# Chunked attention and two dense layers on one core: head order in the loads, GpSimd's share of the first block, and attention ahead of the in-projection

## The chip, the cores and the metric

One core of a Trainium2 chip. The core has TensorE (PE in the profile; its weight loads are PEld), VectorE (DVE), ScalarE (ACT), GpSimd (POOL) and SyncE (SP), which here issues every DMA. The metric is the device time of one execution, in microseconds, as the median of the runs shown.

## The reference

q, k and v have 4 batches, 8 heads, 576 positions and 64 values a head. Attention is computed within chunks of 64 positions only. Its result, heads side by side, is a matrix of 2304 tokens by 512, which goes through two dense layers of the same shape, each with an in-projection to 2048, an activation and an out-projection back to 512:

```
scores = 1/sqrt(64) * (q_c @ k_c.T)          # per batch, head and chunk of 64
attn   = exp(scores - max) / (sum + 1e-9)
x      = (attn @ v_c), heads side by side     # 2304 x 512
x      = gelu_sigmoid(x @ w_in1) @ w_out1     # h * 1/(1+exp(-1.702 h))
out    = mish(x @ w_in2) @ w_out2             # h * tanh(softplus(h))
```

The weights come as 64-bit floats, q, k and v as 32-bit floats.

## The kernel before

Tokens are worked on in six blocks of 384 (three attention tiles of 128 tokens each). A block of a layer has 16 units n, one for each 128 of the 2048 inner columns (f = n % 16). A unit is an in-projection into a PSUM tile h (12 matmuls: four slices of the depth, and for each the products high x high, low x high and high x low of 32-bit numbers split in two, `mm3`), the activation t on ACT, its high part gh and its remainder gl, and two units later (`LAG`) an out-projection of 12 matmuls into the accumulators acc. The first layer's six blocks come first, then the second layer's. The engines' queues are filled in the order in which the code is written (`manual_schedule`), and each engine works strictly in its order.

Weights. Each 64-bit weight tile (512 KB, "raw") is loaded, scaled on ACT (`scale`), put together from its two halves on VectorE in two instructions (`join`, L151 and L152), and split: the high part wi or wo on ACT (L173), the low part by a subtraction (L174), which before stands on GpSimd. One call of `convert` does a split, a join, a scale and further loads for successive tiles. In block 0 of the first layer each unit calls it twice, since every weight is first needed there; the second layer's weights are joined during later blocks and parked in DRAM (`staged`), and split late in the first layer's last block. Raw tiles go through five rotating buffers once the spare ones are used up.

Attention. A tile of 128 tokens is two chunks for eight heads. Its steps are `transposes` of q and k (PSUM tr), the copies qt and kt, `scores` (sc), `shift` (maximum mx and subtraction into e), `exp`, `sums` (sm, rc), `normalize`, `attn_t` (transposes of e, PSUM at) with the copy a, `pv`, then `x_hi` (xh) and `x_lo` (xl), the halves of the layer's input. Matmuls of 64 by 64 use a half of the rows (the row start of the operands) and a half of the columns (the row start of the output). The first three tiles and the first weights follow a list written by hand (`PLAN`); the others are spread over units: f = 1, 6, 11 transposes and the loads of the tile after next, f = 2, 7, 12 scores to normalization, f = 4, 9, 14 attn_t, f = 5, 10, 15 pv to xl. All four PSUM results of a tile share one slot outside the list. In block 0 the normalization and gl stand on GpSimd, in later blocks on VectorE.

Loads. Before, q and k of a tile come in two transfers each (heads 0 to 3, heads 4 to 7, interleaved in SBUF), and v in four of 64 KB, so that each chunk's heads lie in a half of the partitions.

Of the kernel before, what the change touches and what calls it, by code (L numbers as in the profile page):

```python
# [16 lines left out]
P = 128  # L17
# [18 lines left out]
def tile_kernel(  # L36
# [40 lines left out]
    class Weights:  # L77
# [8 lines left out]
        def __init__(self, w_in, w_out, staged):  # L86
# [5 lines left out]
            self.raw, self.f32, self.hi, self.lo = {}, {}, {}, {}  # L92
            self.first, self.ahead = 0, NRAW - 2 if staged else NRAW
# [72 lines left out]
        def split(self):  # L166
# [46 lines left out]
    def load_values(t, i):  # L213

        for c in range(2):
            b, s = divmod(i * P + c * CH, S)
            for r in range(2):
                nc.sync.dma_start(
                    out=t[r * CH : (r + 1) * CH].rearrange("k (p c d) -> k p c d", c=2, d=D)[:, :, c],
                    in_=v[b, r * NP : (r + 1) * NP, s : s + CH, :].rearrange("p k d -> k p d"),  # L220
                )

    class Attention:
# [31 lines left out]
        def scores(self):  # L255
            self.pt = pt = self.psum("sc")
            for p in range(NP):
                for c in range(2):
                    c0 = p * P + c * CH
                    cs = slice(c * CH, (c + 1) * CH)  # L260
                    for r in range(2):
                        rs = slice(r * CH, (r + 1) * CH)
                        nc.tensor.matmul(
                            pt[cs, r, p * CH : (p + 1) * CH],
                            self.qt[rs, c0 : c0 + CH],
                            self.kt[rs, c0 : c0 + CH],
                            start=True,
                            stop=True,
                        )

        def shift(self):
            if self.e is None:
                self.e = at.tile([P, DM], F32, tag="q", name=f"e{self.i}")
            self.eg = self.e.rearrange("p (g k) -> p g k", g=G)
            sv = self.pt[:, :, 0 : NP * CH].rearrange("p r (h k) -> p r h k", h=NP)
            mx = st.tile([P, 2, NP, 1], F32, tag="mx", name=f"mx{self.i}")
            nc.vector.reduce_max(out=mx, in_=sv, axis=AX.X)
            nc.vector.tensor_tensor(
                out=self.e.rearrange("p (h r k) -> p r h k", h=NP, r=2),
                in0=sv,  # L280
                in1=mx.to_broadcast([P, 2, NP, CH]),
# [28 lines left out]
        def pv(self):  # L310
            self.pt = pt = self.psum("pv")
            for p in range(NP):
                for c in range(2):
                    w, o = p % 2, p // 2 * P + c * CH
                    vs = slice((2 * p + c) * D, (2 * p + c + 1) * D)
                    qs = slice(p * P + c * CH, p * P + (c + 1) * CH)
                    for r in range(2):
                        rs = slice(r * CH, (r + 1) * CH)
# [332 lines left out]
```

## Time and profile before

| | |
|---|---|
| median of 3 runs | 895.48 us (894.75 to 896.47) |
| profiled execution, its own time | 894.35 us |
| its span (first to last instruction) | 892.4 us |
| PE busy | 869.9 us, 97% of the span |
| DVE busy | 355.6 us, 40% |
| ACT busy | 276.8 us, 31% |
| POOL busy | 115.0 us, 13% |
| granted TensorE clock, mean | 0.996 of full speed |

Busy shares are means over stages with different limits; the profile also gives them by stretches of time, for each line of the kernel, and as waits with what ended them. A time such as 28.11 counts from the first instruction of the profiled execution.

### The profile page before, as it was taken

The numbers are of one execution on the slowest core, as the hardware profiler recorded it, in microseconds if no ns is written. First come the engines' busy times: TensorE is split into PE (matmuls) and PEld (weight loads), VectorE is DVE, ScalarE is ACT, GpSimd is POOL, SyncE is SP. The second block draws the span as 40 slices with busy tenths as digits, with TensorE's granted clock in tenths as the row PEclk, the third lists the DMA queues.
The fourth block names the chain that finished last, engine by engine and source line by source line (L and its number), as shares of the span: only waits on it lengthen the run. The fifth ranks groups of instructions, "written<-read, shape, count | busy, mean of one in ns | idle before, by whom it ended". The sixth has DMA issues, their size and how long they took to land.

```text
span 892.4 us, 13796 instructions
## 1 busy us (share of the span) xinstructions
PE 869.9 (97%) x5724; PEld 812.1 (91%) x5724; DVE 355.6 (40%) x633; ACT 276.8 (31%) x469; POOL 115.0 (13%) x92
## 2 busy tenths in 40 slices
PE   7878999999999999999999999999999999999998
PEld 5777899999999999999999999999999999999997
DVE  5789744445445455445333222222222222222221
ACT  4777733333334343333434111111111111111111
POOL 2688700000000000000565000000000000000000
PEclk9999999999999999999999999999999999999999
DMA  8957724455336435523342000300200200200000
GB/s 208 284 163 218 213 96 107 107 139 181 117 96 195 125 107 169 153 71 128 112 127 83 1 1 1 107 1 1 106 1 1 107 1 1 107 1 1 36 1 36
DMA packets 93406, 82.69 MB, mean 93 GB/s; under 512 B 60320, under 2 KB 76704, under 8 KB 93344
## 3 DMA queue, kind: packets, MB, share of 16 engines
q1 hardware_dynamic: 93344, 81.81, 31.0%
q8 instruction: 45, 0.74, 0.3%
q14 instruction: 17, 0.14, 0.1%
HBM read 62.39 MB, written 19.40 MB: 92 GB/s over the span
## 4 chain that ended last, share of the span: by engine, by line
PE 88%; DVE 4%; DMA 3%; ACT 2%; SPq 2%; issue 1%; POOL 0%; DVEq 0%; POOLq 0%; ACTq 0%
PE h L345 14%; PE h L343 14%; PE h L344 14%; PE acc L343 7%; PE acc L344 6%; PE acc L345 6%; PE accb L435 5%; PE accb L434 5%; PE accb L433 5%; PE third L434 3%; PE third L435 2%; PE third L433 2%; DVE raw L152 2%; DVE raw L151 2%; PE tr L247 1%
## 5 line engine op out<-in xcount | busy, mean ns | idle before, releaser
L365 DVE CAST gh<-t 128x384 fp32r<-128x384 f32 x176 | 69.3, 394 | 476.0 <-ACT t L413 296.1
L343 PE MATMUL h<-xh,wi 128*128 128x384 f32 x512 | 172.0, 336 | 1.9 <-ACT t L361 1.8
L345 PE MATMUL h<-xh,wi 128*128 128x384 f32 x512 | 171.9, 336 | 0.6 <-POOL wi L174 0.6
L344 PE MATMUL h<-xl,wi 128*128 128x384 f32 x512 | 171.3, 335 | 0.0
L413 ACT ACTIVATE t<-h 128x384 f32<-128x384 f32 x96 | 47.2, 492 | 335.2 <-PE h L345 334.4
L343 PE MATMUL acc<-gh,wo 128*128 128x384 f32 x384 | 134.1, 349 | 0.0
L344 PE MATMUL acc<-gl,wo 128*128 128x384 f32 x384 | 128.6, 335 | 0.0
L345 PE MATMUL acc<-gh,wo 128*128 128x384 f32 x384 | 128.5, 335 | 0.0
L370 DVE TENSOR_TENSOR gl<-t,gh 128x384 fp32r<-128x384 f32 x176 | 98.3, 559 | 11.8
L361 ACT ACTIVATE t<-h 128x384 f32<-128x384 f32 x96 | 47.1, 491 | 172.3 <-PE h L345 81.3
L343 PEld LDWEIGHTS h<-xh,wi 128*128 128x128 f32 x512 | 96.1, 188 | 4.6 <-ACT t L361 3.2
L344 PEld LDWEIGHTS h<-xl,wi 128*128 128x128 f32 x512 | 96.1, 188 | 1.3
L345 PEld LDWEIGHTS h<-xh,wi 128*128 128x128 f32 x512 | 96.1, 188 | 0.9 <-POOL wi L174 0.9
L345 PE MATMUL h<-x2h,wi 128*128 128x384 f32 x256 | 86.4, 337 | 0.0
L343 PE MATMUL h<-x2h,wi 128*128 128x384 f32 x256 | 86.2, 337 | 0.0
L344 PE MATMUL h<-x2l,wi 128*128 128x384 f32 x256 | 86.0, 336 | 0.0
L435 PE MATMUL accb<-wo,gl 128*128 128x512 f32 x192 | 76.2, 397 | 0.0
L434 PE MATMUL accb<-wo,gh 128*128 128x512 f32 x192 | 75.8, 395 | 0.0
L433 PE MATMUL accb<-wo,gh 128*128 128x512 f32 x192 | 74.6, 389 | 0.0
L343 PEld LDWEIGHTS acc<-gh,wo 128*128 128x128 f32 x384 | 72.1, 188 | 2.0
L344 PEld LDWEIGHTS acc<-gl,wo 128*128 128x128 f32 x384 | 72.2, 188 | 0.0
L345 PEld LDWEIGHTS acc<-gh,wo 128*128 128x128 f32 x384 | 72.1, 188 | 0.0
(85 smaller groups left out, 1052.5 us busy)
## 6 DMA issues: line engine op xcount, KB each, us to landing
raw<-in_moe_w_in_dram SPq DMA_DIRECT2D x32, 512.0 KB, 4.1
raw<-in_moe_w_out_dram SPq DMA_DIRECT2D x32, 512.0 KB, 4.0
w_f<-wf SPq DMA_DIRECT2D x32, 256.0 KB, 2.2
ws<-w_f SPq DMA_DIRECT2D x32, 256.0 KB, 2.7
v<-in_v_dram SPq DMA_DIRECT2D x72, 64.0 KB, 2.9
out_dram<-o SPq DMA_DIRECT2D x18, 256.0 KB, 2.1
q<-in_q_dram SPq DMA_DIRECT2D x26, 128.0 KB, 4.2
k<-in_k_dram SPq DMA_DIRECT2D x26, 128.0 KB, 4.3
```

The costliest lines, as they stand in the source:

```text
L151: nc.vector.tensor_scalar(lo, lo, 29, None, op0=ALU.logical_shift_right)
L152: nc.vector.scalar_tensor_tensor(to, hi, 3, lo, op0=ALU.logical_shift_left, op1=ALU.bitwise_or)
L343: nc.tensor.matmul(o, wh, mh, start=start, stop=False)
L344: nc.tensor.matmul(o, wh, ml, start=False, stop=False)
L345: nc.tensor.matmul(o, wl, mh, start=False, stop=stop)
L361: nc.scalar.activation(gt[n], hp.pop(n), AF.Gelu_apprx_sigmoid)
L365: (nc.scalar.copy if n < KF else nc.vector.tensor_copy)(gh[n], gt[n])
L370: eng.tensor_tensor(out=gl[n], in0=gt.pop(n), in1=gh[n].bitcast(F32), op=ALU.subtract)
L413: nc.scalar.activation(gt[n], h, AF.Mish)
L433: nc.tensor.matmul(o, a[:, ts], wh, start=f == 0, stop=False)
L434: nc.tensor.matmul(o, a[:, ts], wl, start=False, stop=False)
L435: nc.tensor.matmul(o, b[:, ts], wh, start=False, stop=f == KF - 1)
```

## The change

Loads: q, k and v of a tile each come in one transfer with the heads in their own order (two where a tile crosses a batch), and v lies by token like q and k. Scores and pv are addressed accordingly: scores take two head pairs to the two halves of the output's partitions, and pv reads a chunk's half of the rows and writes head parity to the halves of the output's partitions. The normalization and gl are on VectorE everywhere, and so is the low part of the first layer's split; that part is held back (`open`) until `rest`, which `convert` calls after its join. In block 0 gl of a unit is held back too (`late`) to the next unit, after its first `convert`. In each unit of the loop the attention step stands ahead of the in-projection. The list `PLAN` and the second layer's splits are as they were.

```diff
         def load_ahead(self):
-            used = self.at["join" if self.staged is not None else "split"]
+            used = self.at["join"] if self.staged is not None else self.at["split"] - len(self.open)
...
             nc.scalar.copy(hi, w)
-            nc.gpsimd.tensor_tensor(out=lo, in0=w, in1=hi.bitcast(F32), op=ALU.subtract)
-            self.hi[key], self.lo[key] = hi, lo
+            self.hi[key] = hi
+            self.open.append((key, w, hi, lo))
+            if self.staged is not None:
+                self.rest()
+
+        def rest(self):
+            eng = nc.vector if self.staged is None else nc.gpsimd
+            while self.open:
+                key, w, hi, lo = self.open.pop(0)
+                eng.tensor_tensor(out=lo, in0=w, in1=hi.bitcast(F32), op=ALU.subtract)
+                self.lo[key] = lo
+
+        def parts(self, key):
+            if key not in self.lo:
+                self.rest()
+            return self.hi[key], self.lo[key]
         def convert(self):
...
             if self.at["scale"] > self.at["join"]:
                 self.join()
+            self.rest()
...
-            for r in range(2):
-                nc.sync.dma_start(
-                    out=t[done : done + n].rearrange("t (p r d) -> t p r d", r=2, d=D)[:, :, r],
-                    in_=src[b, r * NP : (r + 1) * NP, s : s + n, :].rearrange("p t d -> t p d"),
-                )
+            nc.sync.dma_start(
+                out=t[done : done + n].rearrange("p (h d) -> p h d", h=H),
+                in_=src[b, :, s : s + n, :].rearrange("h p d -> p h d"),
+            )
...
-            self.v = at.tile([P, H * D], F32, tag="v", name=f"v{self.i}")
-            load_values(self.v, self.i)
+            self.v = load_tok(at, "v", v, self.i)
...
-            for p in range(NP):
+            for u in range(NP // 2):
                 for c in range(2):
-                    c0 = p * P + c * CH
-                    cs = slice(c * CH, (c + 1) * CH)
-                    for r in range(2):
...
-                            pt[cs, r, p * CH : (p + 1) * CH],
+                    o = (u * 2 + c) * CH
+                    for w in range(2):
+                        c0 = (2 * u + w) * P + c * CH
+                        for r in range(2):
...
+                                pt[w * CH : (w + 1) * CH, r, o : o + CH],
...
-                    w, o = p % 2, p // 2 * P + c * CH
...
+                    cs = slice(c * CH, (c + 1) * CH)
                     for r in range(2):
-                        rs = slice(r * CH, (r + 1) * CH)
+                        h = 2 * p + r
+                        o = (r * NP // 2 + p // 2) * P + p % 2 * CH
                         nc.tensor.matmul(
-                            pt[w * D : (w + 1) * D, r, o : o + CH],
-                            self.v[rs, vs],
-                            self.a[rs, qs],
+                            pt[r * D : (r + 1) * D, c, p * CH : (p + 1) * CH],
+                            self.v[cs, h * D : (h + 1) * D],
+                            self.a[cs, o : o + CH],
...
-        eng = nc.gpsimd if n < KF else nc.vector
-        eng.tensor_tensor(out=gl[n], in0=gt.pop(n), in1=gh[n].bitcast(F32), op=ALU.subtract)
+        nc.vector.tensor_tensor(out=gl[n], in0=gt.pop(n), in1=gh[n].bitcast(F32), op=ALU.subtract)
...
-            "U": lambda i: tiles[i].normalize(pool),
+            "U": lambda i: tiles[i].normalize(nc.vector),
...
         for n in range(4, N + LAG):
             f = n % KF
-            if n < NA:
-                j = n // KF
-                hp[n] = in_proj(W[0], (xh[j], xl[j]), f)
-                if n < KF:
-                    W[0].convert()
-                gelu(n)
-                g_hi(n)
-                g_lo(n)
...
             if n < NA - KF and f > 0:
...
+            if n < NA:
+                j = n // KF
+                hp[n] = in_proj(W[0], (xh[j], xl[j]), f)
+                if n < KF:
+                    W[0].convert()
+                while late:
+                    g_lo(late.pop())
+                gelu(n)
+                g_hi(n)
+                if n < KF:
+                    late.append(n)
+                else:
+                    g_lo(n)
```

What that does to VectorE's queue in the hand-written list, around the normalization of the second and third tile (e_201 is the second tile's e after the change, e_first the third's in both). Before, from the third tile's maximum on:

```order
L277 TENSOR_REDUCE mx_251<-sc_226 128x8
L278 TENSOR_TENSOR e_first<-sc_226,mx_251 128x2x4x64
L151 TENSOR_SCALAR raw_174<-raw_174 128x512
L152 SCALAR_TENSOR_TENSOR raw_174<-raw_174 128x512
L291 TENSOR_REDUCE sm_286<-e_first 128x8
L292 TENSOR_SCALAR sm_286<-sm_286 128x8
L293 RECIPROCAL rc_287<-sm_286 128x8
L151 TENSOR_SCALAR raw_203<-raw_203 128x512
L152 SCALAR_TENSOR_TENSOR raw_203<-raw_203 128x512
L151 TENSOR_SCALAR raw_221<-raw_221 128x512
L152 SCALAR_TENSOR_TENSOR raw_221<-raw_221 128x512
L339 TENSOR_TENSOR xl_387<-pv_315,xh_386 128x4x128
```

After, the same place from the first join on (maximum and shift of the third tile stand ahead of it as before; lines of the changed file):

```order
L152 TENSOR_SCALAR raw_168<-raw_168 128x512
L153 SCALAR_TENSOR_TENSOR raw_168<-raw_168 128x512
L301 TENSOR_REDUCE sm_274<-e_first 128x8
L302 TENSOR_SCALAR sm_274<-sm_274 128x8
L303 RECIPROCAL rc_275<-sm_274 128x8
L152 TENSOR_SCALAR raw_197<-raw_197 128x512
L153 SCALAR_TENSOR_TENSOR raw_197<-raw_197 128x512
L152 TENSOR_SCALAR raw_212<-raw_212 128x512
L153 SCALAR_TENSOR_TENSOR raw_212<-raw_212 128x512
L307 TENSOR_TENSOR e_201<-e_201,rc_237 128x512
L307 TENSOR_TENSOR e_first<-e_first,rc_275 128x512
L348 TENSOR_TENSOR xl_366<-pv_300,xh_365 128x2x4x64
```

The second tile's normalization, which was GpSimd's next instruction after the reciprocal, now stands on VectorE behind the third tile's shift, three joins and a sum.

VectorE in unit 5, the first with a pv in the loop. Before, xl and a run of joins:

```order
L339 TENSOR_TENSOR xl_732<-pv_714,xh_731 128x4x128
L151 TENSOR_SCALAR raw_612<-raw_612 128x512
L152 SCALAR_TENSOR_TENSOR raw_612<-raw_612 128x512
L151 TENSOR_SCALAR raw_652<-raw_652 128x512
L152 SCALAR_TENSOR_TENSOR raw_652<-raw_652 128x512
```

After, each join is followed by the subtraction of a split (wi, wo), and once a unit by a gl:

```order
L348 TENSOR_TENSOR xl_677<-pv_659,xh_676 128x2x4x64
L152 TENSOR_SCALAR raw_583<-raw_583 128x512
L153 SCALAR_TENSOR_TENSOR raw_583<-raw_583 128x512
L185 TENSOR_TENSOR wi_693<-raw_363,wi_693 128x512
L378 TENSOR_TENSOR gl_701<-t_635,gh_637 128x384
L152 TENSOR_SCALAR raw_631<-raw_631 128x512
L153 SCALAR_TENSOR_TENSOR raw_631<-raw_631 128x512
L185 TENSOR_TENSOR wo_719<-raw_583,wo_719 128x512
```

A split's subtraction stands one join behind the join of its own weight, and xl moved ahead of one join more.

ACT in unit 4, which has the copy a. Before, a stands behind the unit's gelu (t) and gh:

```order
L173 CAST wi_646<-raw_380 128x512
L141 ACTIVATE raw_384<-raw_384 128x512
L361 ACTIVATE t_654<-h_633 128x384
L365 CAST gh_656<-t_654 128x384
L308 COPY a_665<-at_660 128x512
```

After, a is the first instruction of the unit:

```order
L318 COPY a_610<-at_605 128x512
L174 CAST wi_625<-raw_359 128x512
L142 ACTIVATE raw_363<-raw_363 128x512
L370 ACTIVATE t_635<-h_612 128x384
L374 CAST gh_637<-t_635 128x384
```

The copies qt and kt, exp and xh moved in the same way in their units.

## Rows read from the trace of the kernel before

**Rows 1.** The page: busy time (parts 1) and a load's landing (part 6).
```profile
PE 869.9 (97%) x5724; PEld 812.1 (91%) x5724; DVE 355.6 (40%) x633; ACT 276.8 (31%) x469; POOL 115.0 (13%) x92
...
raw<-in_moe_w_in_dram SPq DMA_DIRECT2D x32, 512.0 KB, 4.1
```
**Rows 2.** Busy time by stretches: PE, PEld, DVE, ACT, POOL, PEclk, DMA share, GB/s.
```profile
28.11:43.75 15.64, 14.26 (x107) 12.99 (x106) 12.63 (x13) 13.65 (x23) 10.95 (x9) 1.00 1.06 328
43.75:54.34 10.59, 7.07 (x42) 6.43 (x41) 10.11 (x10) 7.33 (x12) 10.12 (x8) 1.00 0.58 143
54.34:82.31 27.97, 24.45 (x197) 23.03 (x197) 24.69 (x28) 21.54 (x38) 21.21 (x16) 1.00 0.68 199
82.31:110.00 27.69, 24.55 (x197) 23.10 (x197) 23.62 (x24) 20.55 (x36) 21.82 (x17) 1.00 0.78 222
```
**Rows 3.** The chain in block 1, 130 to 165 us: start, us, what.
```profile
133.47 0.44 PE at L303 x4
138.08 0.67 PE pv L319 x30
...
148.19 0.62 PE sc L263 x32
...
161.95 0.67 PE pv L319 x30
```
**Rows 4.** TensorE's waits, 0 to 120 us: us in total, times, longest.
```profile
PE pv L319 <- ACT a L308: 4.2, 3, 1.8
PE tr L247 <- DVE xl L339: 2.8, 2, 1.4
...
PE tr L247 <- DMA k<-in_k_dram: 1.1, 1, 1.1
```
**Rows 5.** Groups by line, VectorE, 0 to 122 us: busy us, mean ns.
```profile
L152 DVE SCALAR_TENSOR_TENSOR raw<-raw 128x512 int32<-128x512 int32 x32 | 40.1, 1252 | 3.5 <-ACT raw L141 0.9
L151 DVE TENSOR_SCALAR raw<-raw 128x512 int32<-128x512 int32 x32 | 29.9, 935 | 1.8 <-DMA raw<-in_moe_w_in_dram 1.8
```
**Rows 6.** Groups by line, VectorE, 122 to 420 us.
```profile
L370 DVE TENSOR_TENSOR gl<-t,gh 128x384 fp32r<-128x384 f32 x63 | 35.2, 559 | 2.2
...
L152 DVE SCALAR_TENSOR_TENSOR wf<-raw 128x512 int32<-128x512 int32 x32 | 22.2, 693 | 1.2
L151 DVE TENSOR_SCALAR raw<-raw 128x512 int32<-128x512 int32 x32 | 13.5, 421 | 0.0
...
L297 DVE TENSOR_TENSOR e<-e,rc 128x512 f32<-128x512 f32 x12 | 8.3, 692 | 0.4
```
**Rows 7.** Timeline of VectorE, 62.6 to 64 us: start, us, instruction.
```profile
62.70 0.42 DVE L151 TENSOR_SCALAR raw<-raw 128x512 int32<-128x512 int32 x1
63.22 0.69 DVE L152 SCALAR_TENSOR_TENSOR raw<-raw 128x512 int32<-128x512 int32 x1
63.83 1.54 DVE L151 TENSOR_SCALAR raw<-raw 128x512 int32<-128x512 int32 x1
```
**Rows 8.** Timeline of GpSimd, 61 to 66 us.
```profile
63.56 1.53 POOL L174 TENSOR_TENSOR wi<-raw,wi 128x512 fp32r<-128x512 f32 x1 [1.33 <-ACT wi L173]
```
**Rows 9.** Groups by line, GpSimd, 0 to 122 us.
```profile
L174 POOL TENSOR_TENSOR wi<-raw,wi 128x512 fp32r<-128x512 f32 x16 | 24.5, 1531 | 10.8 <-ACT wi L173 10.8
```
**Rows 10.** Timeline of GpSimd, 13 to 17 us.
```profile
14.92 1.04 POOL L297 TENSOR_TENSOR e<-e,rc 128x512 f32<-128x512 f32 x1 [0.41 <-DVE rc L293]
```
**Rows 11.** Timeline of TensorE, 15.9 to 23 us.
```profile
16.13 1.04 PE L303 MATMUL at<-ident,e 128*128 128x128 f32 x8
19.69 1.59 PE L319 MATMUL pv<-a,v 64*64 64x64 f32 x32 [2.52 <-DMA v<-in_v_dram]
```
**Rows 12.** Timeline of SyncE's DMA issues, 12 to 34 us.
```profile
12.81 7.17 SPq L218 DMA_DIRECT2D v<-in_v_dram  x8
```
**Rows 13.** Busy time by stretches, columns as in the second group.
```profile
18.00:22.00 4.00, 2.31 (x36) 2.14 (x36) 3.01 (x7) 2.43 (x5) 1.84 (x2) 0.69 0.53 112
```
**Rows 14.** Groups by line, ScalarE, 0 to 122 us.
```profile
L173 ACT CAST wi<-raw 128x512 fp32r<-128x512 f32 x16 | 10.6, 665 | 13.4 <-DVE raw L152 13.4
```

More of the change, by code (lines that the diff above doesn't have):

```diff
@@ L92, in __init__ @@
             self.raw, self.f32, self.hi, self.lo = {}, {}, {}, {}
+            self.open = []
             self.first, self.ahead = 0, NRAW - 2 if staged else NRAW
@@ L205, in load_into @@
             n = min(P - done, S - s)
-            for r in range(2):
-                nc.sync.dma_start(
-                    out=t[done : done + n].rearrange("t (p r d) -> t p r d", r=2, d=D)[:, :, r],
-                    in_=src[b, r * NP : (r + 1) * NP, s : s + n, :].rearrange("p t d -> t p d"),
-                )
-            done += n
-    def load_values(t, i):
-        for c in range(2):
-            b, s = divmod(i * P + c * CH, S)
-            for r in range(2):
[L218 to L221, printed above, removed]
+            nc.sync.dma_start(
+                out=t[done : done + n].rearrange("p (h d) -> p h d", h=H),
+                in_=src[b, :, s : s + n, :].rearrange("h p d -> p h d"),
+            )
+            done += n
     class Attention:
@@ L256, in scores @@
             self.pt = pt = self.psum("sc")
-            for p in range(NP):
+            for u in range(NP // 2):
                 for c in range(2):
-                    c0 = p * P + c * CH
-                    cs = slice(c * CH, (c + 1) * CH)
-                    for r in range(2):
-                        rs = slice(r * CH, (r + 1) * CH)
-                        nc.tensor.matmul(
-                            pt[cs, r, p * CH : (p + 1) * CH],
[L265 to L269, printed above, removed]
+                    o = (u * 2 + c) * CH
+                    for w in range(2):
+                        c0 = (2 * u + w) * P + c * CH
+                        for r in range(2):
+                            rs = slice(r * CH, (r + 1) * CH)
+                            nc.tensor.matmul(
+                                pt[w * CH : (w + 1) * CH, r, o : o + CH],
+                                self.qt[rs, c0 : c0 + CH],
+                                self.kt[rs, c0 : c0 + CH],
+                                start=True,
+                                stop=True,
+                            )
         def shift(self):
@@ L274, in shift @@
             self.eg = self.e.rearrange("p (g k) -> p g k", g=G)
-            sv = self.pt[:, :, 0 : NP * CH].rearrange("p r (h k) -> p r h k", h=NP)
-            mx = st.tile([P, 2, NP, 1], F32, tag="mx", name=f"mx{self.i}")
+            sv = self.pt[:, :, 0 : G // 2 * CH].rearrange("p r (g k) -> p r g k", k=CH)
+            mx = st.tile([P, 2, G // 2, 1], F32, tag="mx", name=f"mx{self.i}")
             nc.vector.reduce_max(out=mx, in_=sv, axis=AX.X)
             nc.vector.tensor_tensor(
-                out=self.e.rearrange("p (h r k) -> p r h k", h=NP, r=2),
+                out=self.e.rearrange("p (r g k) -> p r g k", r=2, k=CH),
                 in0=sv,
-                in1=mx.to_broadcast([P, 2, NP, CH]),
+                in1=mx.to_broadcast([P, 2, G // 2, CH]),
                 op=ALU.subtract,
@@ L332, in x_hi @@
             sl = slice(self.t * P, (self.t + 1) * P)
-            self.x = self.pt[:, :, 0 : NP * CH].rearrange("p r (a t) -> p r a t", t=P)
-            self.xo = [x[j][:, :, sl].rearrange("p (r a) t -> p r a t", r=2) for x in (xh, xl)]
+            self.x = self.pt[:, :, 0 : NP * CH].rearrange("p c (a t) -> p c a t", a=NP)
+            self.xo = [x[j][:, :, sl].rearrange("p a (c t) -> p c a t", c=2) for x in (xh, xl)]
             copy(self.xo[0], self.x)
@@ L348, in in_proj @@
         h = ps.tile([P, TB], F32, tag="h", name=f"h{f}")
-        a, b = w.hi["i", f], w.lo["i", f]
+        a, b = w.parts(("i", f))
         for kk in range(KD):
@@ L380, in out_a @@
         a, b = gh.pop(n), gl.pop(n)
-        wh, wl = W[0].hi["o", f], W[0].lo["o", f]
+        wh, wl = W[0].parts(("o", f))
         for m in range(KD):
@@ L482, in load_v @@
             tiles[i].v = half_slot(f"v{i}", w1.room(f"v{i}"))
-            load_values(tiles[i].v, i)
+            load_into(tiles[i].v, v, i)
         def keep_warm(n):
@@ L496, in split, with join @@
                 w1.load_ahead()
-        act, vec, pool = nc.scalar.copy, nc.vector.tensor_copy, nc.gpsimd
+        def join():
+            w1.join()
+            w1.rest()
+        act, vec = nc.scalar.copy, nc.vector.tensor_copy
         steps = {
@@ L504, in tile_kernel @@
             "c": lambda _: w1.scale(),
-            "j": lambda _: w1.join(),
+            "j": lambda _: join(),
             "s": lambda _: split(),
@@ L515, in tile_kernel @@
             "N": lambda i: tiles[i].sums(),
-            "U": lambda i: tiles[i].normalize(pool),
-            "u": lambda i: tiles[i].normalize(nc.vector),
+            "U": lambda i: tiles[i].normalize(nc.vector),
             "A": lambda i: tiles[i].attn_t(),
@@ L536, in tile_kernel @@
         att = tiles[TT]
-        nxt, done = tiles[TT + 1], 2
+        nxt, done, late = tiles[TT + 1], 2, []
         for n in range(4, N + LAG):
             f = n % KF
-            if n < NA:
-                j = n // KF
-                hp[n] = in_proj(W[0], (xh[j], xl[j]), f)
-                if n < KF:
-                    W[0].convert()
-                gelu(n)
-                g_hi(n)
-                g_lo(n)
-            elif n < N:
-                mish(n, in_proj(W[1], x2[order_b[n // KF - NB]], f))
             if n < NA - KF and f > 0:
@@ L566, in tile_kernel @@
                     att.sums()
-                    att.normalize(pool if n < KF else nc.vector)
+                    att.normalize(nc.vector)
                 elif at_step == 3:
@@ L575, in tile_kernel @@
                     att = nxt
+            if n < NA:
[11 more added lines that the diff above has]
+                    g_lo(n)
+            elif n < N:
+                mish(n, in_proj(W[1], x2[order_b[n // KF - NB]], f))
             m = n - LAG
```

3 lines of the change are left out of this document (removed).

## The prediction

> **What bounds the kernel now.** First the page: TensorE is busy 97% of the span [rows 1], so a change can pay only where TensorE still waits. The table by stretches says where: between 28.11 us (first in-projection) and 110 us it is busy 14.26 of 15.64, 7.07 of 10.59, 24.45 of 27.97 and 24.55 of 27.69 us [rows 2]; these 11.6 us are half of the 22.5 that it is idle in the span, and the rest lies ahead of them and in the program's tail. Everything to be won therefore lies in block 0, the 16 units in which the weights of the first layer are still being converted. How much: the chain of block 1 is TensorE alone, and there five units with one attention tile take from pv at 138.08 to pv at 161.95, which is 23.87 us [rows 3]. The two such stretches of block 0 (pv to pv) take 27.97 and 27.69 [rows 2]: 4.1 and 3.8 us of waiting. From transposes of e to pv block 1 needs 4.61 us [rows 3], of which 0.44 is the transposes, so one group of 12 matmuls costs (4.61 - 0.44) / 2 = 2.09. The stretch 43.75 to 54.34 holds one group more than that, 6.70 against 10.59: 3.9 us lost. 28.11 to 43.75 holds six groups and one scores, 13.2 against 15.64: 2.4 us. Together **14.2 us**, the most that block 0 can give behind its first matmul.
>
> Who keeps TensorE waiting? Directly ACT's copy of a and VectorE's xl [rows 4]; but VectorE is busy 10.11 of 10.59, 24.69 of 27.97 and 23.62 of 27.69 us, and GpSimd 10.12, 21.21 and 21.82 [rows 2]. So TensorE waits for a conversion pipeline whose two engines are nearly full. And VectorE is full of work that it does slowly: its two join instructions take 1252 and 935 ns each in block 0 [rows 5], and 693 and 421 ns later, for the second layer, when GpSimd is idle [rows 6]. Inside block 0 one sees it switch: a join at 62.70 takes 0.42 + 0.69; the next, at 63.83, takes 1.54 for the first half alone [rows 7], and between the two, at 63.56, GpSimd began a split [rows 8].
>
> **The change part by part.**
>
> *GpSimd out of block 0.* VectorE gets back 32 x (1.252 - 0.693) + 32 x (0.935 - 0.421) = 34.3 us [rows 5, 6]. It takes on 32 subtractions for the splits, 16 gl and 6 normalizations. A gl on VectorE is 0.559, a normalization 0.692 [rows 6]. The split of 512 columns is not shown on VectorE: 0.559 (the same operation on 384 columns) bounds it below, 0.693 (the join's second half, which reads the same strided buffer) above; I take 0.692, the form nearest to it. Sum 32 x 0.692 + 16 x 0.559 + 6 x 0.692 = 35.2. So VectorE's work stays what it was, to within 1 us, and the hops over GpSimd, 1531 ns for a split [rows 9], go. What then sets the pace is VectorE's queue against TensorE's. A join takes 1.13 start to start (62.70 to 63.83) and successive independent instructions overlap by 0.08 (63.22 + 0.69 against 63.83) [rows 7], so a split costs 0.61 and a gl 0.48. Five units hold ten joins, ten splits, five gl, one tile's maximum, subtraction, wait for exp, sum, two small ones and normalization (about 3.75) and one xl (0.61): 11.3 + 6.1 + 2.4 + 3.75 + 0.6 = **24.2 us** against TensorE's 23.87 and today's 27.8. VectorE stays the narrower of the two by a hair, and TensorE should lose some tenths per five units in place of 4 us.
>
> I walked the new order of VectorE's queue from the first in-projection on with these durations beside TensorE's groups. TensorE then waits about 0.5 us for the split of the fourth in-projection weight, 0.7 for the first loop tile's normalization, and 0.8 and 0.6 for the gl behind the two later score steps, where VectorE has the tile's 3.75 us on top: **2.6 us** in all. Two things the walk does not resolve: ACT's exp sits behind a table load and may keep VectorE 0.5 us longer in each of two tiles, and a raw load may come late once; I put 1.5 us for them.
>
> *The start.* GpSimd normalizes the second tile at 14.92 in parallel with VectorE [rows 10]; in the new queue that instruction stands behind the third tile's maximum and shift (1.3), three joins (3.4) and a sum (1.1). With the first tile's own normalization (0.6) it starts at about 14.9 + 0.6 + 5.8 = 21.3 and ends at 21.9. TensorE does the transposes of tiles 0 and 1 back to back at 16.13 and waits for v until 19.69 for the first pv [rows 11]; now the second half of those transposes, and every pv behind it, starts at 21.9, pv at 22.4. That is 2.7 us late. The first in-projection follows 8.4 us behind that pv today, through waits for ACT, VectorE and the k of tile 3 (1.1 us, [rows 4]), so the 2.7 lie on its path only in part: I put a third, 0.9, with nothing and 2.7 as bounds. Against that stands the issue: 12 transfers of q and k become 6, and eight issues of v that hold the queue for 7.17 us [rows 12] become two. The DMA engines are only 0.53 busy from 18 to 22 us [rows 13], while the queue is still issuing, so what follows comes earlier by up to some 2 us. I take the start as **0.7 us later**, between 2.7 later and 0.4 earlier. From 18 to 22 us the granted clock is down to 0.69 [rows 13] because TensorE had nothing to do; the new gap there is longer and I expect the same, hidden under the same waits.
>
> *Attention ahead of the in-projection.* TensorE's groups are the same; between pv and the next unit's transposes there are two groups (4.2 us) before and after. What changes is ACT's and VectorE's queues: xh, xl and the copies of q, k and a now come ahead of gelu. That is what the two waits of [rows 4] are about (a 4.2, xl 2.8 us), and it is part of the 14.2. In later blocks TensorE never waits, so there it is worth nothing; the first unit of a block also gets its last tile one group earlier, which costs nothing there either.
>
> *Quadrants.* Scores now take 0.62 and pv 0.67 per tile [rows 3]. Scores already alternate over both halves of rows and columns and stay as they are. pv goes from two quadrants per head pair to four. At best it becomes like scores, 0.05 x 15 = 0.7 us; at worst its matmuls stop overlapping in pairs, which doubles it. I take 0, with -0.7 and +10 as bounds.
>
> Sum: 14.2 - 2.6 - 1.5 - 0.7 = 9.4 us. The profiled execution took 894.35 us (span 892.40), 1.13 under the median of 895.48; taken off the median the sum gives **886.1 us**.
>
> **The rivals.**
>
> *TensorE-bound block 0.* If splits cost nearer 0.56 and the start is not late, VectorE is never behind: 14.2 + 0.4 + 0.7 at the very best, 15 us, 880.5. For it: 32 splits x 0.13 = 4 us of slack. Against: the heavy score steps cannot be smoothed out.
>
> *Weights late.* A raw buffer is free when its split is done; the unit that needs its next contents comes four joins, three splits and a gl or two later, 6.4 to 7.3 us. A load takes 4.1 to land [rows 1], with issue and scaling 5.3. Where a tile's 768 KB of q, k, v are ahead of it in the queue (3.5 us at the 222 GB/s of the last stretch in [rows 2]), it is 8.8: 1.4 or more late, for three tiles 4.2: 890.3. For it: the DMA share was already 0.78 [rows 2], and the same bytes now come in 13% less time. Against: the loads fall just ahead of the step in which VectorE has 3.75 us of attention.
>
> *VectorE waits at every split.* The split's subtraction needs ACT's copy, and in VectorE's strict queue everything stands behind it: joins, gl, xl. GpSimd could wait alone. The copy takes 0.665 [rows 14]; if each of the 29 later splits waited for a whole one, 19.3 us: slower, 896.4 with half of it and 905 with all. It decides at 0.32 us per split. Against: between the join of a weight and its split stand another split and join, 1.74 us, and ACT is busy only 20.55 of 27.69 [rows 2] (85% of 24.2). For: ACT also has gelu, exp and two table loads in line.
>
> *pv serial.* In the new order two neighbours share the row half. If neighbours then run one behind the other, pv costs 0.67 more, in 15 tiles 10 us: 896. Against: scores of two column halves with one row half follow each other at one place removed and still finish in 0.62 [rows 3]. The Trainium skill speaks for this rival: "TensorE: Matmul & The Clock Gate", Part 3 (packing small matmuls), says that a weight load overlaps matmuls in flight only when the row group differs, by which half of the new neighbours would stall; no run here shows such an order yet, and by that rule alone the time would be the 896 just given.
>
> *No effect.* If the long joins came of something else than GpSimd, nothing is given back and VectorE gets 35 us more. [rows 7, 8] speak against it; it goes with the slower cases.
>
> **How the numbers follow.** Chances: as forecast (884 to 889.5) 0.54; TensorE-bound (880.5 to 884) 0.14; weights late or other stalls (889.5 to 893.5) 0.17; pv serial 0.04, about no change; slower by the split queue or no effect 0.07; something that takes all of it and no more 0.04. A difference under 0.2% (1.8 us) is about what a measurement of this kernel cannot tell from none. Faster 0.84, same 0.09, slower 0.07. The range from 881.5 to 892.5 leaves out the far end of the TensorE-bound case and all from 892.5 up, about 2 in 10; the forecast's own range is 884 to 889.5.
>
> **What would show it.** In the new profile: both join lines at 0.42 and 0.69 throughout block 0, no GpSimd there, VectorE still over 90% busy from 30 to 97 us, its last split near 98, and TensorE without waits from about 102 instead of 110. pv to pv in block 0 should be 24 to 25 us. The first in-projection starts at 28 to 29, with the second tile's normalization behind three joins. It is wrong if joins stay long, if VectorE shows idle time before its split lines (released by ACT), if ACT's scaling waits for DMA, or if pv in later blocks exceeds 0.7 us.

## The result, and the profile after

The changed kernel takes **885.08 us** (median, 884.82 to 885.80) against 895.12 us of the kernel before in the same measurement: a ratio of 0.9888 with a 95% interval of 0.9871 to 0.9905, 10.0 us less. The profiled execution's span is 883.0 us against 892.4.

From the page of the changed kernel, busy time, then the landing of the raw weights (KB each, median us from issue to landing):

```profile
PE 867.3 (98%) x5724; PEld 810.6 (92%) x5724; DVE 353.2 (40%) x687; ACT 277.9 (31%) x469; POOL 41.4 (5%) x38
...
raw<-in_moe_w_in_dram SPq DMA_DIRECT2D x32, 512.0 KB, 4.5
```

VectorE is as busy as before [rows 1], with 54 instructions more: what the joins gave back paid for them. The groups by line on VectorE, 0 to 122 us, which answer to [rows 5, 6] (busy us, mean ns of one | idle before, and what ended it):

```profile
L153 DVE SCALAR_TENSOR_TENSOR raw<-raw 128x512 int32<-128x512 int32 x32 | 22.2, 694 | 2.4
L152 DVE TENSOR_SCALAR raw<-raw 128x512 int32<-128x512 int32 x32 | 13.5, 421 | 0.0
L378 DVE TENSOR_TENSOR gl<-t,gh 128x384 fp32r<-128x384 f32 x20 | 11.1, 554 | 2.8 <-ACT gh L374 2.7
L185 DVE TENSOR_TENSOR wo<-raw,wo 128x512 fp32r<-128x512 f32 x16 | 11.0, 686 | 1.0 <-ACT wo L174 0.8
L185 DVE TENSOR_TENSOR wi<-raw,wi 128x512 fp32r<-128x512 f32 x16 | 11.0, 685 | 0.3 <-ACT wi L174 0.3
```

The joins take in block 0 what they took in later blocks before, and 32 splits together wait 1.1 us for ACT. The stretches that answer to [rows 2] (PE, PEld, DVE, ACT, POOL, PEclk, DMA share, GB/s): first in-projection to first pv of the loop, and twice pv to pv.

```profile
28.04:50.02 21.98, 18.83 (x136) 17.40 (x134) 19.53 (x38) 19.39 (x33) 0.00 (x0) 1.00 0.87 266
50.02:74.68 24.66, 24.10 (x198) 23.07 (x197) 22.81 (x44) 22.40 (x40) 0.00 (x0) 1.00 0.82 242
74.68:99.57 24.89, 24.09 (x197) 23.06 (x196) 22.38 (x43) 21.10 (x37) 0.00 (x0) 1.00 0.83 244
```

Pv to pv is 24.66 and 24.89 us in place of 27.97 and 27.69. What TensorE still waits for, 0 to 120 us (us in total, times, longest; compare [rows 4]):

```profile
PE at L313 <- DVE e L307: 5.8, 2, 4.8
PE acc L353 <- DVE gl L378: 1.4, 2, 0.8
...
PE h L354 <- DVE wi L185: 1.2, 1, 1.2
...
PE h L353 <- DVE xl L348: 0.9, 1, 0.9
```

The 4.8 us lie at the start. TensorE's timeline from 15.9 us, beside [rows 11]:

```profile
15.93 0.60 PE L313 MATMUL at<-ident,e 128*128 128x128 f32 x4
21.34 1.08 PE L313 MATMUL at<-ident,e 128*128 128x128 f32 x4 [4.81 <-DVE e L307]
22.35 1.13 PE L328 MATMUL pv<-a,v 64*64 64x64 f32 x32
...
28.04 0.42 PE L352 MATMUL h<-xh,wi 128*128 128x384 f32 x1
```

The first pv is 2.66 us later than before, and yet the first in-projection starts at the same time (28.04 against 28.11): something else made up for it. Last, the chain in block 1 (compare [rows 3]):

```profile
127.60 0.62 PE pv L328 x32
...
137.63 0.62 PE sc L273 x32
```

Pv on four quadrants takes exactly what scores take, 0.62 in place of 0.67.

### The profile page after: what moved, and what is told of

It is laid out like the page before. It is cut to its first block, busy times and chain, and to the rows that moved or that the text cites. A ratio compares the mean times of both kernels' runs of the same rounds, so it can differ in the third digit from the quotient of the medians.

```text
span 883.0 us, 13566 instructions
## 1 busy us (share of the span) xinstructions
PE 867.3 (98%) x5724; PEld 810.6 (92%) x5724; DVE 353.2 (40%) x687; ACT 277.9 (31%) x469; POOL 41.4 (5%) x38
## 4 chain that ended last, share of the span: by engine, by line
PE 91%; DVE 6%; ACT 2%; DMA 1%; issue 0%; DVEq 0%; ACTq 0%
PE h L352 15%; PE h L354 14%; PE h L353 14%; PE acc L354 7%; PE acc L353 7%; PE acc L352 7%; PE accb L443 5%; PE accb L442 5%; PE accb L441 5%; PE third L442 3%; PE third L443 3%; PE third L441 2%; DVE raw L153 1%; PE tr L256 1%; PE pv L328 1%; PE sc L273 1%
## 5 line engine op out<-in xcount | busy, mean ns | idle before, releaser
L352 PE MATMUL h<-xh,wi 128*128 128x384 f32 x512 | 177.3, 346 | 0.0
L354 PE MATMUL h<-xh,wi 128*128 128x384 f32 x512 | 171.6, 335 | 1.2 <-DVE wi L185 1.2
L354 PE MATMUL acc<-gh,wo 128*128 128x384 f32 x384 | 128.6, 335 | 0.0
L352 PE MATMUL acc<-gh,wo 128*128 128x384 f32 x384 | 128.3, 334 | 0.0
L378 DVE TENSOR_TENSOR gl<-t,gh 128x384 fp32r<-128x384 f32 x192 | 107.2, 558 | 14.8 <-ACT gh L374 2.7
```

Of the source, the lines that this page charges most:

```text
L352: nc.tensor.matmul(o, wh, mh, start=start, stop=False)
L354: nc.tensor.matmul(o, wl, mh, start=False, stop=stop)
L378: nc.vector.tensor_tensor(out=gl[n], in0=gt.pop(n), in1=gh[n].bitcast(F32), op=ALU.subtract)
```

## The experiments

The change has three parts, called here G (GpSimd out of block 0), A (attention ahead of the in-projection) and L (loads in one transfer, with the layout and the quadrants that follow from it). All eight combinations were measured, and six more edits of the changed kernel. For all of them the table gives three places of their profiles: the start of the first in-projection; from there to the end of the 15th out-projection (that of unit f = 14, which ends at 108.80 us in the changed kernel), called block 0 below; and the issue of the first raw weight behind the fourth tile's v. The last column is the ratio to the kernel before, measured beside it, with its 95% interval. The three places are read from one profiled execution each, whose own time differs from the median by 1.9 us in the tenth run, by 0.8 and 0.7 in the eighth and third, and by 0.6 or less in the others.

| kernel | median us | first in-proj. | to 15th out-proj. | raw issue | ratio |
|---|---|---|---|---|---|
| before | 894.4 to 895.1 | 28.11 | 89.07 | 27.26 | 1 |
| G (fifth) | 891.08 | 29.18 | 85.54 | 28.33 | 0.9955 (0.9942 to 0.9967) |
| A (sixth) | 894.56 | 28.19 | 89.96 | 26.97 | 0.9998 (0.9989 to 1.0006) |
| L (seventh) | 890.00 | 25.12 | 88.30 | 21.09 | 0.9948 (0.9935 to 0.9960) |
| A, L (first) | 891.02 | 25.26 | 89.33 | 21.51 | 0.9954 (0.9942 to 0.9967) |
| G, L (second) | 884.54 | 27.40 | 80.92 | 23.95 | 0.9887 (0.9874 to 0.9901) |
| G, A (third) | 888.98 | 29.82 | 82.93 | 29.11 | 0.9934 (0.9921 to 0.9946) |
| changed: G, A, L | 885.08 | 28.04 | 80.75 | 24.63 | 0.9888 (0.9871 to 0.9905) |
| many transfers (ninth) | 887.14 | 27.05 | 84.16 | 26.77 | 0.9914 (0.9899 to 0.9928) |
| second e early (eighth) | 884.20 | 27.82 | 81.15 | 21.00 | 0.9877 (0.9862 to 0.9893) |
| both e early (eleventh) | 882.34 | 25.13 | 80.77 | 21.48 | 0.9864 (0.9850 to 0.9879) |
| the same without A (twelfth) | 882.94 | 25.25 | 81.22 | 21.25 | 0.9872 (0.9855 to 0.9888) |
| reads on GpSimd (fourth) | 912.49 | 27.37 | 109.07 | 23.90 | 1.0198 (1.0184 to 1.0212) |
| writes on GpSimd (tenth) | 885.41 | 27.98 | 83.34 | 24.37 | 0.9900 (0.9884 to 0.9916) |

The theory was the prediction's: what pays is that VectorE no longer works beside GpSimd. The rivals gave the gain to the order of the attention, or to the loads.

**First: without G.** The low parts of the splits, gl and the normalizations of block 0 go back to GpSimd, and nothing is held back.

```diff
-            eng = nc.vector if self.staged is None else nc.gpsimd
+            eng = nc.gpsimd
...
-                if n < KF:
-                    late.append(n)
-                else:
-                    g_lo(n)
+                g_lo(n)
```

> The changed kernel with GpSimd's work put back (low parts of the splits, gl and normalizations of block 0), attention still ahead of the in-projection and loads and quadrants as changed. Theory (the gain is that VectorE no longer works beside GpSimd): VectorE's joins in block 0 are back at about 1250 and 935 ns, pv to pv in block 0 at 27 to 28 us, time 892 to 896. Rival one (the order of the attention is what paid): joins long but the waits of a and xl gone, 886 to 889. Rival two (loads paid): as rival one, about 888 to 891.

891.02 us, 1.0 us under the theory's range and at the far end of rival two's. VectorE's groups by line, 0 to 122 us:

```profile
L153 DVE SCALAR_TENSOR_TENSOR raw<-raw 128x512 int32<-128x512 int32 x32 | 42.8, 1336 | 2.9 <-ACT raw L142 0.2
L152 DVE TENSOR_SCALAR raw<-raw 128x512 int32<-128x512 int32 x32 | 32.1, 1003 | 0.0
```

The long joins are back, and block 0 takes 89.33 us from the first in-projection, 8.6 more than in the changed kernel. But the first in-projection comes at 25.26, 2.8 us earlier, which the theory had not priced. G is worth 5.9 us here, less than the whole.

**Second: without A.** The two blocks of the loop change places again; nothing else.

```diff
-            if n < NA - KF and f > 0:
-                at_step = (f - 1) % 5
...
             if n < NA:
                 j = n // KF
...
+            if n < NA - KF and f > 0:
+                at_step = (f - 1) % 5
```

> The changed kernel with the attention step behind the in-projection again, all else as changed. Theory (VectorE's pace decides, the order hardly counts): joins stay at 421 and 694 ns, pv to pv in block 0 within 0.6 us of 24.8, time 885 to 888. Rival one (the order is what paid): TensorE waits for a, xl and e return with 1 to 2 us each in three tiles, 890 to 894.

884.54 us, within 0.6 us of the changed kernel: 0.5 us under the theory's range and far from the rival's, so the order is not what paid. TensorE's waits, 0 to 120 us, show 1.5 us of waits for a in place of the one for the fourth tile's e:

```profile
PE at L313 <- DVE e L307: 4.7, 1, 4.7
PE pv L328 <- ACT a L318: 1.5, 2, 1.1
```

**Third: without L.** Loads, scores, pv and the addressing of xh as before.

```diff
-            self.v = load_tok(at, "v", v, self.i)
+            self.v = at.tile([P, H * D], F32, tag="v", name=f"v{self.i}")
+            load_values(self.v, self.i)
```

> The changed kernel with loads, scores and pv of before. Theory (loads and quadrants are worth their 0.05 us per tile and little else): pv 0.67 instead of 0.62, first in-projection near 28, time 885.5 to 887. Rival two (fewer transfers give time at the start and for the weights): first in-projection 1 to 2 us later or raw loads late, 887.5 to 891.

888.98 us: the theory, which gave the loads 0.05 us a tile, falls; rival two is right. SyncE's issues (start, us, instruction) show where the weights lose their time. Without L:

```profile
13.27 8.24 SPq L235 DMA_DIRECT2D v<-in_v_dram  x8
21.55 0.60 SPq L116 DMA_DIRECT2D raw<-in_moe_w_out_dram  x1
...
24.04 0.92 SPq L224 DMA_DIRECT2D k<-in_k_dram  x2
25.00 4.06 SPq L235 DMA_DIRECT2D v<-in_v_dram  x4
29.11 0.60 SPq L111 DMA_DIRECT2D raw<-in_moe_w_in_dram  x1
```

In the changed kernel:

```profile
10.79 2.95 SPq L223 DMA_DIRECT2D v<-in_v_dram  x2
13.78 4.34 SPq L116 DMA_DIRECT2D raw<-in_moe_w_out_dram  x1
...
23.58 0.37 SPq L223 DMA_DIRECT2D k<-in_k_dram  x1
24.00 0.57 SPq L223 DMA_DIRECT2D v<-in_v_dram  x1
24.63 1.52 SPq L111 DMA_DIRECT2D raw<-in_moe_w_in_dram  x1
```

Eight issues of v hold the queue 8.24 us and two hold it 2.95, but the raw weight behind the two holds it 4.34 us where it takes 0.60 behind the eight, so 1.6 us of that are left. The fourth tile's k, which the eleventh experiment shows to hang on the first pv, comes at 24.04 and 23.58, nearly at the same time. Most of the 4.5 us by which the weights behind are earlier (24.63 against 29.11) lies after it: four issues of the fourth tile's v hold the queue 4.06 us, one holds it 0.57.

**Fourth: GpSimd works, but nobody waits for it.** In the changed kernel, after each split of the first layer:

```diff
                 self.lo[key] = lo
+                if self.staged is None:
+                    h = hi.bitcast(F32)[:, 0:TB]
+                    for _ in range(2):
+                        nc.gpsimd.tensor_tensor(out=zeros, in0=h, in1=h, op=ALU.subtract)
```

> The changed kernel with 64 subtractions of 128 x 384 on GpSimd in block 0, two after each split, which read that split's high part and write into a tile that nobody reads afterwards: no instruction of another engine waits for them. Theory (two engines at work side by side slow each other): before, 74 us of GpSimd lengthened VectorE's joins by 34.3 us, 0.46 us for each; 64 x about 1.2 us would lengthen VectorE's work by some 35 us, the joins to 0.8 to 1 and 1.1 to 1.3 us, and since VectorE sets the pace of block 0 the time to 905 to 925. Rival (joins were long because of handing over between the engines, not because of work beside them): joins 421 and 694 ns, time 885 to 886.

912.49 us, 27.4 more than the changed kernel and in the theory's range; the joins are a little shorter than it said. VectorE's groups, 0 to 150 us:

```profile
L153 DVE SCALAR_TENSOR_TENSOR raw<-raw 128x512 int32<-128x512 int32 x32 | 31.2, 975 | 2.4
L152 DVE TENSOR_SCALAR raw<-raw 128x512 int32<-128x512 int32 x32 | 23.6, 737 | 0.0
L185 DVE TENSOR_TENSOR wi<-raw,wi 128x512 fp32r<-128x512 f32 x16 | 15.5, 971 | 0.3 <-ACT wi L174 0.3
L382 DVE TENSOR_TENSOR gl<-t,gh 128x384 fp32r<-128x384 f32 x20 | 15.4, 772 | 1.6 <-ACT gh L378 1.5
...
L305 DVE TENSOR_REDUCE sm<-e 128x8 f32<-128x512 f32 x6 | 4.1, 682 | 2.1 <-ACT e L300 2.1
L352 DVE TENSOR_TENSOR xl<-pv,xh 128x512 fp32r<-128x512 f32 x6 | 4.0, 681 | 2.0 <-ACT xh L348 2.0
```

And GpSimd's, 0 to 140 us:

```profile
L190 POOL TENSOR_TENSOR zeros<-wo 128x384 bf16<-128x384 f32 x32 | 32.4, 1012 | 18.2 <-ACT wo L174 16.2
L190 POOL TENSOR_TENSOR zeros<-wi 128x384 bf16<-128x384 f32 x32 | 30.7, 960 | 46.8 <-PE idle L500 24.2 <-ACT wi L174 21.1
```

No instruction of another engine waits for these; they lengthen VectorE's joins, wi and gl alone by 9.0 + 10.1 + 4.6 + 4.4 = 28 us for 63 us of GpSimd. Over the whole program VectorE is busy 386.0 us against 353.2, 33 us more. That is the prediction's main step by itself: working side by side is enough to cost this time, with nothing handed over. The reduction (682 ns) and xl, one of whose inputs lies in PSUM (681), are as in the changed kernel (682 and 687).

**Fifth to seventh: one part alone**, made of the edits of the first three (the fifth without A and L, the sixth without G and L, the seventh without G and A).

> Only GpSimd's part of the change on the kernel before (loads, quadrants and order of the attention as before). Theory (the parts add up: the order is worth nothing, the loads 3.9 us as the third experiment's difference says): 888 to 890. Rival (the order counts as soon as raw loads are late): 890.5 to 893.

> Only the order of the attention changed on the kernel before. Theory (the order is worth nothing whichever engine works): 894 to 896. Rival (the order takes away the waits for a and xl, 7.0 us in the table of waits before, where VectorE is slow): 890 to 892.5.

> Only the loads and quadrants changed on the kernel before. Theory (the loads are worth 3.9 us as with the other parts): 890 to 892. Rival (beside a slow VectorE an earlier weight is worth nothing but the 0.05 us per pv): 893.5 to 895.

G alone gives 3.6 us, in the rival's range and short of the theory's; A alone gives nothing and L alone 4.6 us, both as by the theory. With G there, L gives 6.5 (fifth against second), and with L there, G gives 5.5 (seventh against second). By the medians the two together give 10.0 us where they give 8.2 apart; the intervals of the three ratios are too wide to show these 1.8 us, but the profiles point the same way. By the table, G shortens block 0 by 3.5 us without L and by 7.4 with it, and delays the first in-projection by 1.1 and 2.3. L brings the first in-projection forward by 3.0 us without G and 1.8 with it, and shortens block 0 by 0.8 and by 4.6, perhaps because a VectorE that has caught up needs the weights sooner: in the fifth run its joins wait 1.3 us for loads. If A gains anywhere it is with G and without L (891.08 to 888.98), and there too some runs of the two overlap, as they do in the other three pairs. In the sixth run the waits for a and xl of [rows 4] did become smaller, but another took their place (TensorE's waits, 0 to 122 us):

```profile
PE at L323 <- POOL e L317: 4.0, 1, 4.0
PE pv L339 <- ACT a L328: 2.7, 2, 2.0
```

**Eighth: the second tile's normalization early.** In the list, U1 directly behind N1:

```diff
-... S2 U0 c N1 c M2 j w17 ... v1 l U1 U2 A1
+... S2 U0 c N1 U1 c M2 j w17 ... v1 l U2 A1
```

> The changed kernel with the second tile's normalization on VectorE directly behind that tile's sum and reciprocal, ahead of the third tile's maximum and three joins. Theory (it holds TensorE for 4.8 us and, through it, the issue of the fourth tile's k and all weights behind it, at 23.6 us where the first experiment has 20.5): no wait for that e, first in-projection at 25 to 26.5, time 882.3 to 884. Rival (the conversion pipeline is what block 0 is paced by, and what is won at the start is waited for later): first in-projection earlier, the third pv of the loop at 99 as before, time 884.6 to 885.6.

884.20 us, between the two ranges; the profile shows the rival's late pv (the third of the loop at 99.74), and another reason for it. TensorE, 16 to 25 us:

```profile
16.21 1.04 PE L313 MATMUL at<-ident,e 128*128 128x128 f32 x8
19.17 0.69 PE L328 MATMUL pv<-a,v 64*64 64x64 f32 x32 [1.92 <-DVE sm L302]
22.30 1.09 PE L313 MATMUL at<-ident,e_first 128*128 128x128 f32 x4 [2.44 <-DVE e_first L307]
```

The first wait is gone (pv waits 1.92 behind it) and the first pv 3.2 us earlier; then the third tile's normalization, still behind the joins, holds TensorE for 2.44, and the first in-projection starts at 27.82.

**Ninth: many transfers, new layout.** q and k go in two halves by heads (`parts` 2), v in four quarters; bytes, layout, scores and pv stay as changed.

```diff
+            for r in range(parts):
+                h0, h1 = r * H // parts, (r + 1) * H // parts
...
-                out=t[done : done + n].rearrange("p (h d) -> p h d", h=H),
-                in_=src[b, :, s : s + n, :].rearrange("h p d -> p h d"),
+                    out=t[done : done + n, h0 * D : h1 * D].rearrange("p (h d) -> p h d", d=D),
+                    in_=src[b, h0:h1, s : s + n, :].rearrange("h p d -> p h d"),
```

> The changed kernel with its new layout and quadrants, but q and k of a tile in two transfers each and v in four of 64 KB, by heads. Theory (what the loads pay is issue time on SyncE's queue: 8.2 us for eight issues of v in the third experiment against 2.95 for two): raw loads of the weights issued 4 us later than in the changed kernel, time 887.5 to 889. Rival (layout and quadrants are what pays): 885 to 886.

887.14 us, just under the theory's range, 2.1 above the changed kernel and 1.8 below the third: about half of L's 3.9 us is the number of issues, the rest layout and quadrants. The raw weights are issued 2.1 us later than in the changed kernel, not 4: by heads, eight issues of v and the four of the fourth tile are cheaper than in the third run, which is a part of that rest:

```profile
12.43 6.40 SPq L225 DMA_DIRECT2D v<-in_v_dram  x8
...
23.65 3.08 SPq L225 DMA_DIRECT2D v<-in_v_dram  x4
26.77 0.47 SPq L111 DMA_DIRECT2D raw<-in_moe_w_in_dram  x1
```

Another part lies behind block 0: from the 15th out-projection to TensorE's last matmul the kernels with the old pv take 771.44 us, those with the new one 770.56, 0.9 less.

**Tenth: GpSimd only writes**, but for a copy of one value a partition behind each split, which puts the fills in their place.

```diff
+                    nc.gpsimd.tensor_copy(out=zeros[:, 0:1], in_=hi.bitcast(F32)[:, 0:1])
+                    for _ in range(4):
+                        nc.gpsimd.memset(zeros, 0.0)
```

> The changed kernel with GpSimd writing only: after each split one element of it copied, then four fills of 128 x 384 two-byte values. The Trainium skill (SBUF, State Buffer, Who interferes with whom) says that a VectorE instruction with two inputs from SBUF is held up by a GpSimd instruction that reads SBUF and not by one that only writes. By that rule the second join instruction stays at 0.69, the split at 0.69, gl at 0.55, and the first join instruction, with one input, may still be held up; time 885 to 890. Rival (any work on GpSimd slows VectorE in proportion to its busy time, as in the fourth experiment, 0.5 us for each): all three longer by the same share, time up by about 0.4 us per us of GpSimd.

885.41 us, no difference from the changed kernel. VectorE, 0 to 122 us:

```profile
L153 DVE SCALAR_TENSOR_TENSOR raw<-raw 128x512 int32<-128x512 int32 x32 | 22.2, 694 | 2.4
L152 DVE TENSOR_SCALAR raw<-raw 128x512 int32<-128x512 int32 x32 | 14.5, 454 | 0.0
```

GpSimd, in the same stretch:

```profile
L190 POOL MEMSET zeros<- 128x384 bf16 x128 | 57.9, 452 | 7.4
```

Beside 58 us of fills, and 10.6 us of the copies of one value, the second join instruction stays at 694 ns, and the first is 33 ns longer. (This is the profile that lies 1.9 us above its median, so its 83.34 in the table is no measure of the median.)

**Eleventh and twelfth: both normalizations early**, with A and without.

```diff
-... U0 c N1 c M2 j w17 l v0 A0 X2 N2 V0 c c j j v1 l U1 U2 A1
+... U0 c N1 U1 c M2 j w17 l v0 A0 X2 N2 U2 V0 c c j j v1 l A1
```

> The changed kernel with the second and the third tile's normalization on VectorE directly behind their reciprocals, ahead of the joins. Theory (after the eighth experiment: block 0 is paced by the conversion of weights, whatever the start): the third tile's wait of 2.4 us gone, first in-projection at 25.5 to 26.5, the last pv of block 0 still at 99 to 100, time 884 to 885.5. Rival (two joins later are what the first in-projections wait for): 885.5 to 887.

> The changed kernel with both normalizations early as in the run beside it, and the attention behind the in-projection as before the change. Theory (neither counts): 884 to 885.5. Rival (they add up to something): 882.5 to 884.

882.34 us (ahead of both its ranges) and 882.94 (in the rival's). The first in-projection is at 25.13, and all that follows keeps the 2.9 us: the last pv of block 0 comes at 96.68, against 99.57. So the theory that block 0 is paced by the conversion whatever the start is false. SyncE's issues in the eleventh:

```profile
20.43 0.37 SPq L223 DMA_DIRECT2D k<-in_k_dram  x1
...
21.48 1.94 SPq L111 DMA_DIRECT2D raw<-in_moe_w_in_dram  x1
```

The fourth tile's k goes into the buffer of the first tile's a, which pv reads; an earlier pv starts the k, and the queue behind it, 3.15 us sooner. The eighth run had the early k too, without the early first in-projection, and gained under 1 us by the median. No run has the early first in-projection without the early queue, so what either is worth by itself is not shown. The eleventh kernel is the best found: its runs (881.95 to 883.51) lie below all of the changed kernel's.

## Why the prediction was right, and where it was not

The forecast, 886.1, is 1.0 us from the measured 885.08, and the side is right. Of its steps:

- **VectorE's joins** (34.3 us given back beside GpSimd): right to 2 ns, and shown to be a matter of working side by side by the fourth run.
- **What VectorE takes on** (0.692 a split, 0.559 a gl, 0.692 a normalization): measured 0.686, 0.554 and 0.690. Pv to pv was to be 24 to 25 us and is 24.66 and 24.89; the two waits for gl behind the score steps were walked as 0.8 and 0.6, which they are.
- **Ahead of the first pv of the loop**, 6.3 us were lost before, and 1.2 were to remain. By the order of the code pv now stands one group of 2.09 us earlier; so the gain there is 26.23 - 21.98 - 2.09 = 2.2 us, and 4.1 remain. The waits for the fourth in-projection's weight and the first normalization are 1.2 and 1.0 in place of 0.5 and 0.7, xl's 0.9 was not in the walk, and TensorE is busy 1.0 us more than my count of groups. The allowance of 1.5 us for exp and a late load did not occur where I put it; it happened to cover half of the difference.
- **The start**, 0.7 us later by the sum, is 0.1 earlier, out of two terms that were both mis-sized. The step that failed is "the 2.7 lie on its path only in part: I put a third, 0.9": the eleventh run brings the first in-projection forward by 2.9 us, and the time by 2.7, when both normalizations come early, so all of it lay on the path. With the loads of before a third would have been about right: there G delays the first pv by 2.5 us and the first in-projection by 1.1 (kernel before against fifth run), with the new loads by 2.4 and 2.3 (seventh against second). And the shorter queue, "earlier by up to some 2 us" of which the sum kept almost nothing, brings the first in-projection forward by 3.0 us alone. The two cancel.
- **Pv on four quadrants**, taken at 0, gained about 0.9 us behind block 0, a little more than the near bound of 0.7.
- **Attention ahead of the in-projection** was counted in the 14.2; it is worth nothing measurable here.

Summed by place: 0.1 at the start, 2.2 up to the first pv of the loop, 3.3 + 2.8 between pv and pv, 0.9 behind block 0, together 9.3 of the 9.4 by which the span became shorter. The total is this close in part by luck: 2.9 us were missing ahead of the first pv of the loop and 0.4 between pv and pv, and the allowance of 1.5, the 0.8 at the start and the 0.9 of pv made up for them. So the size was right, and the attribution was not: the loads, which I priced inside the start, carry 4.6 us alone and 6.5 with G, at least as much as GpSimd does (3.6 alone, 5.5 with L).

Of the rivals, VectorE waiting at every split is out (1.1 us in 32 splits; half a copy at each of 29 splits would by the prediction's own sum have given 895.8, not the 896.4 that it names). No effect is out by the joins, and block 0 is not bound by TensorE alone, since pv to pv is still 0.8 and 1.0 us above block 1's 23.87. Weights late is half seen: one of its signs came, for ACT's scaling waits for loads four times in the loop, 3.3 us in all and at most 1.05 at once; but VectorE's joins wait for no load in the changed kernel, while in the fifth run, without L, they wait 1.3 us.

Pv serial is out at 0.62 us: the Trainium skill's rule ("TensorE: Matmul & The Clock Gate", Part 3) would have had neighbours with one row group hold each other up, and in this case the new order with such neighbours is as fast as the scores without them; the measurement decides.

The granted clock was 0.50 (1.2 GHz, the lower of its two levels) from 20 to 24 us, behind the gap of 4.8 us, and 0.50 in the same stretch before the change, there behind a gap of 2.5 us; two tiles' transposes of e and two pv from 21.34 to 25.52 took 4.2 us against 2.1 by block 1's rows, and before, two pv and one tile's transposes from 19.69 to 23.37 took 3.7 against 1.8, so it cost about the same in both.

## What to carry to other kernels

When an engine is full, look first whether its instructions have one duration throughout: two lines at 1252 and 935 ns that take 694 and 421 elsewhere say that a neighbour costs half of them, and moving the neighbour's work onto the slowed engine may then be free. At the start of a program, count what one serial queue issues and what each step there waits for; a delay ahead of the first in-projection can be passed on in full, as it was here, and it may reach the loads through a buffer that a late matmul still reads. A sum that comes out right proves none of its terms: here each part had to be run alone and with the others, since two parts gave 3.6 and 4.6 us alone and 10.0 together.

## What the runs showed of the hardware

GpSimd instructions that read SBUF cost VectorE about half of their own time (34.3 us of joins beside 74.7 us of GpSimd before the change, 28 of joins, wi and gl, 33 of all VectorE's work, beside 63 in the fourth run), and fills, which only write, cost 1.0 us of joins beside 58. Not every VectorE instruction is hit: reductions and subtractions with an input in PSUM keep their 0.68 to 0.69 us. The Trainium skill ("SBUF — State Buffer", Who interferes with whom) says so: a VectorE instruction with two inputs from SBUF is held up by GpSimd instructions that read SBUF, and not by those that only write; both runs agree with it for the second join instruction, the splits and gl. The first join instruction has one input and is hit as well: 421 ns become 737 beside the reading instructions and 454 beside the fills. Eight issues of v by chunk held SyncE's queue 8.24 us in the third run and 7.17 in the kernel before, eight of the same size by heads 6.40, two for the same bytes 2.95; the single issue behind the two then held it 4.34.
